# A new written-out order and a three-piece last store in an attention and token/channel-mixer kernel

## The chip, the cores and the metric

The kernel runs on one core of one Trainium2 chip. The metric is the device time of one execution in microseconds; three runs of a version give a median.

## The reference

Blockwise causal attention over 8 batches, 8 heads, 576 positions and 64 channels, followed by a mixer: a token part that multiplies along the positions, and a channel part that multiplies along the 512 channels, each with a residual.

```python
scores = scale * np.matmul(q, k.transpose(0, 1, 3, 2))       # masked by blocks of 64
attn = np.exp(scores - max); attn = attn / (sum + 1e-09)
x = np.matmul(attn, v)                                       # heads side by side: (8, 576, 512)
h = np.maximum(x.transpose(0, 2, 1) @ w_tok1, 0.0) @ w_tok2
u = x + h.transpose(0, 2, 1)
out = u + np.maximum(u @ w_ch1, 0.0) @ w_ch2
```

## The kernel before

The kernel is built in two steps. First the Python code adds about 1,500 numbered operations to a plan; an operation is a bundle of instructions on one engine with its dependencies and, for matmuls, the PSUM banks that it takes. Then the string `ORDER` is walked word by word, and each word emits one operation. A word is a number, an engine letter (T is TensorE, A ScalarE, D VectorE, P GpSimd, S SyncE) and the letters of the banks taken: `41Ta` is operation 41 on TensorE in bank a. Each engine works through its own words in the order written and stops at the first whose inputs or bank are not there. So `ORDER` is the whole schedule. An operation that may run on one of two engines (an evacuation of PSUM on ScalarE or VectorE, a clearing on VectorE or GpSimd) gets its engine from the word too.

What the operations do, by number, so far as they are spoken of below:

- 0A loads the exponential's table. 1D to 6D fill parts of the value tiles, 8D and 9D parts of the token weights, 7D fills `zeros` (part of the tile that the profile calls `wd_sb`), all at L339.
- 41T is eleven matmuls on `zeros`, 512 columns each (L364), which need 7D. 42T to 78T are single matmuls on `zeros` (L372) whose results nobody reads; 42, 46, 50 and so on to 78 have 256 columns, the others 512. Only those that `ORDER` names are emitted. They need 7D and a free bank.
- 11S and 14S load the two halves of the first keys by SyncE's queue, 12A and 15A cast them, 13D and 16D transpose them. 18D, 20D and 22D transpose the three parts of the first queries.
- Batch 0 has its own form of attention: the score sets 98T, 105T, 122T, 102T, 158T, 142T, 125T, 162T, 138T, 145T, 165T (L562) write pairs of banks called s and t (98T two single banks more), and one exponential on 1024 columns (L580) empties a pair: 99A, 106A, 123A, 103A, 159A, 143A, 126A, 163A, 139A, 146A, 166A. 118A and 119A (L736) empty the two single banks of 98T. When 166A has run, the pairs' space turns into four single banks e to h.
- The heads' products with the values are L616 (107T to 175T for batch 0) and L669 (the last 64 positions, 155T for instance); VectorE divides them by the sums (L642, L697).
- Batch 1 begins with the score sets 202T, 208T and 241T in single banks, each emptied by four exponentials of 512 columns (L777). 202T takes banks b, e, f, g.
- Later batches' queries, keys and values come by GpSimd's queue (L417, L469) and are transposed on VectorE (L440). 355P is a load of values, 519P and 522P load four heads' keys and queries of batch 3, 520D and 521D transpose the first. 201 and 240 clear parts of an exponential's result (L599), 240 after the exponentials 236 to 239. 258T is a product with its division 259D and 260D; 426T is the token product of that batch.
- The channel part runs in `channel_up_half`, `channel_up_fast` and `channel_down_fast` with seven products in place of eight (L1114, L1238, L1372); VectorE adds what the banks hold to `o_sb` (L1396), and stores follow at L1438 by SyncE's queue, or ScalarE's for the last batch.

In `channel_down_fast` a batch is worked in one go (`joint`), but the last in two halves of its token chunks, `c0 == 0` and `c0 == 1`. `row` is one of the two rows of `o_sb`, and `h0:h1` says which of the two column halves a store takes. The last operation of `ORDER` before is 1503S, a store of both column halves of one row for `c0 == 0`; the product 1500T and the addition 1501D stand right ahead of it.

Of the kernel before, what the change touches and what calls it, by code (L numbers as in the profile page):

```python
# [27 lines left out]
class Plan:  # L28
# [78 lines left out]
    272D 285Tg 280A 276D 195Tedcf 198A 197A 4D 282D 5D 286D 283Th 284D 310Ta 319Tg 287Th 288A 316Td 295Tc 317T 318D  # L107
    320T 196A 243A 322Th 323T 321A 199A 228Tdbeg 324A 200D 289Tf 207D 290T 232A 230A 261D 296T 297A 6D 345D 311T
    312D 231A 191P 229A 192P 301Tb 193P 262D 346P 302T 235Tcghe 239A 291A 236A 292Td 293T 233D 190P 194P 201P 344D
    304Te 294D 305T 348D 234D 298Tc 299T 347D 352P 216Td 219Tf 220D 237A 303A 217D 218D 213Tb 222Tg 306A 214D 223D  # L110
    300A 238A 215D 240D 225Tc 226D 224D 367Tdhea 370A 227D 221D 313Tb 314T 369A 255Tc 315D 373Tfgeh 246Tb 368A 247D
    376A 307Td 308T 354D 377A 256D 248D 257D 375A 91P 249Te 250D 251D 334Th 371A 360Tcbag 364A 309D 263D 374A 92P
    372D 338Te 339T 335T 349P 362A 353D 252Tb 350D 361A 351D 363A 258Ta 393Tcfgd 397A 395A 396A 93P 336T 355P 264D
    253D 259D 260D 254D 394A 426Tb 427A 406Tagfd 337D 519P 522P 409A 521D 428Tc 340T 410A 407A 520D 400Tadfb 429A
    430Tc 408A 523D 356P 325Tg 94D 341D 358P 359P 402A 524D 431D 365P 366P 404A 357P 384Tb 385D 387Tc 95D 440Td 441A
    381Te 403A 525P 386D 326T 401A 388D 534P 528P 378Tb 389D 379D 390Td 536Tcafh 540A 537A 382D 383D 391D 380D 392D
    434Te 405P 435D 529D 539A 327T 432Td 549Tbfec 433D 685P 552A 398P 399P 553A 328D 438Th 551A 423Td 424D 425D 538A
    436Tg 437D 442Tc 526D 688P 533P 329Td 443A 446Tg 444Tc 417Ta 96D 418D 531P 411Tf 330T 412D 550A 413D 530D 445A
# [60 lines left out]
def kernel(  # L179
# [1148 lines left out]
    def channel_down_fast(b, g_done, wc2_ready, u_done, prio):  # L1328
        gt, ut = g_of(b), u_of(b)
        joint = b != B - 1  # L1330
# [12 lines left out]
        for ts in ((0, 1),) if joint else ((0,), (1,)):  # L1343
            c0, nt = ts[0], len(ts)
# [90 lines left out]
            pieces = [(0, 0, 2), (1, 0, 2)] if c0 == 0 else [(0, 0, 2), (1, 1, 2), (1, 0, 1)]  # L1435
# [151 lines left out]
```

## Time and profile before

| | |
|---|---|
| median of three runs | 285.12 us |
| lowest, highest | 284.26 us, 285.19 us |
| the profiled execution, its own time | 285.85 us |
| its span in the profile | 284.1 us |
| TensorE busy, share of the span | 277.7 us, 98% |
| VectorE busy | 242.4 us, 85% |
| ScalarE busy | 176.0 us, 62% |

The profile's span goes from the first to the last instruction of the program; the profiled execution's own time has 1.75 us more around it. In a timeline row the first number is the start in microseconds, the second the length, then engine, line, operation, what is written and read, and how many such instructions stand together; brackets tell the idle time ahead of it and what ended that. Several matmuls in one row overlap, so the row's length is the spacing of all but the last plus the whole latency of the last. PEld is the loading of weights for a matmul, and an engine's name with a q is its queue of instructions.

### The profile page before, as it was taken

Reading aid. Unit: us, or ns where it says so; the run is one execution under the profiler, and the core shown is the slowest. Engines: PE = TensorE matmul, PEld = TensorE weight load, DVE = VectorE, ACT = ScalarE, POOL = GpSimd, SP = SyncE. Lnnn points to the kernel's source line nnn. Section 1 sums busy time; section 2 is a strip of 40 time slices with the busy share of each in tenths; the row PEclk is TensorE's granted clock in tenths of the full one; section 3 lists DMA queues with packets and bytes.
Section 4 is the critical chain, followed back from the end, with each engine's and each line's share of the span. In section 5 each row is a group of like instructions: output and inputs, shape, how many; then the busy total and the mean of one; then the engine's idle time right before and its main releaser. Section 6 shows DMA issues by size and latency. Waiting matters only on the chain.

```text
span 284.1 us, 8556 instructions
## 1 busy us (share of the span) xinstructions
PE 277.7 (98%) x3586; PEld 194.4 (68%) x3586; DVE 242.4 (85%) x527; ACT 176.0 (62%) x320; POOL 80.2 (28%) x133
## 2 busy tenths in 40 slices
PE   7999999999999999999999999999999999999994
PEld 2457665567767876887777649744488755788883
DVE  4579598889999999989988999879996979889884
ACT  3697896768798666798979891244545774530000
POOL 8876563633742313092552320000000000000000
PEclk9999999999999999999999999999999999999999
DMA  8999999969959578499999827020123600012264
GB/s 158 164 166 196 189 202 206 167 88 111 147 71 166 115 134 105 76 116 87 161 98 253 71 41 96 29 66 18 37 39 71 227 0 1 2 74 95 103 152 171
DMA packets 64773, 31.74 MB, mean 112 GB/s; under 512 B 53088, under 2 KB 55904, under 8 KB 64736
## 3 DMA queue, kind: packets, MB, share of 16 engines
q0 software_dynamic: 45040, 17.64, 53.7%
q1 hardware_dynamic: 19408, 13.05, 17.7%
q8 instruction: 28, 0.46, 0.6%
q10 hardware_dynamic: 288, 0.52, 0.5%
q14 instruction: 9, 0.07, 0.1%
HBM read 35.85 MB, written 9.44 MB: 159 GB/s over the span
## 4 chain that ended last, share of the span: by engine, by line
PE 89%; DMA 6%; POOL 1%; DVE 1%; issue 1%; ACT 1%; POOLq 0%
PE mm L1372 17%; PE late L1372 9%; PE mm L1238 7%; PE late L1114 7%; PE mm L1114 7%; PE late L1238 6%; PE mm L562 5%; PE late L616 4%; PE late L562 3%; PE mm L814 3%; PE mm L616 3%; PE late L1463 3%; PE mm L1041 3%; DMA gT<-in_k_dram 2%; PE mm L913 2%; PE late L814 2%
## 5 line engine op out<-in xcount | busy, mean ns | idle before, releaser
L777 ACT ACTIVATE e_sb<-late 128x512 bf16<-128x512 f32 x85 | 48.4, 609 | 11.5 <-PE late L562 7.3
L777 ACT ACTIVATE e_sb<-mm 128x512 bf16<-128x512 f32 x83 | 47.5, 607 | 7.7 <-PE mm L562 3.3
L440 DVE STREAM_TRANSPOSE qk_sb<-qk_sb 128x288 int32<-128x288 int32 (+2 forms) x57 | 37.0, 693 | 4.5 <-ACT qk_sb L393 1.9
L469 POOL DMA_DIRECT2D vals<-in_v_dram x45 | 37.1, 838 | 7.7 <-DMA wc_sb<-in_moe_w_ch_dram 2.5
L1372 PEld LDWEIGHTS <-gT 128*128 128x128 bf16 x288 | 27.8, 98 | 4.6
L1372 PEld LDWEIGHTS <-sums 128*128 128x128 bf16 x288 | 27.8, 98 | 4.0 <-DVE gT L1354 0.4
L562 PE MATMUL mm<-qk_sb 32*64 32x320 bf16 (+6 forms) x462 | 26.8, 274 | 0.6 <-issue 0.6
L562 PEld LDWEIGHTS <-qk_sb 32*64 32x64 bf16 (+1 forms) x1024 | 16.8, 100 | 15.0 <-issue 9.8
L616 PEld LDWEIGHTS <-e_sb 128*128 128x128 bf16 x640 | 23.5, 97 | 4.4 <-issue 1.1
L562 PE MATMUL late<-qk_sb 32*64 32x320 bf16 (+6 forms) x454 | 25.2, 276 | 0.0
L1114 PEld LDWEIGHTS <-ws_sb 128*128 128x128 bf16 x192 | 18.0, 98 | 3.9 <-issue 0.9
L599 POOL MEMSET e_sb<- 64x512 bf16 (+1 forms) x22 | 11.4, 522 | 29.2 <-ACT e_sb L777 19.0
L1114 PEld LDWEIGHTS <-wc_sb 128*128 128x128 bf16 x144 | 15.5, 114 | 1.5
L1238 PEld LDWEIGHTS <-ws_sb 128*128 128x128 bf16 x96 | 9.4, 98 | 9.7
L1372 PE MATMUL mm<-wd_sb,sums 128*128 128x256 bf16 x126 | 15.6, 273 | 0.0
L616 PE MATMUL late<-vals,e_sb 128*128 128x65 bf16 x330 | 14.4, 193 | 0.0
L642 DVE TENSOR_TENSOR x_sb<-late,rinv 128x256 bf16<-128x256 f32 x33 | 13.6, 419 | 0.7
L580 ACT ACTIVATE e_sb<-sc 128x1024 bf16<-128x1024 f32 x11 | 10.8, 1030 | 5.2 <-PE sc L562 5.0
L616 PE MATMUL mm<-vals,e_sb 128*128 128x65 bf16 x310 | 13.8, 193 | 0.0
L800 ACT ACTIVATE gT<-late 128x512 bf16<-128x512 f32 x18 | 10.6, 606 | 5.0 <-PE late L1114 2.8
L393 ACT COPY late<-mm 128x512 f32<-128x512 f32 x16 | 9.2, 578 | 7.2 <-PE mm L1238 3.7
L642 DVE TENSOR_TENSOR x_sb<-mm,rinv 128x256 bf16<-128x256 f32 x31 | 12.6, 415 | 0.5
(202 smaller groups left out, 645.7 us busy)
## 6 DMA issues: line engine op xcount, KB each, us to landing
out_dram<-o_sb SPq DMA_DIRECT2D x14, 512.0 KB, 3.3
vals<-in_v_dram POOLq DMA_DIRECT2D x28, 128.0 KB, 5.3
qk_sb<-in_k_dram POOLq DMA_DIRECT2D x12, 288.0 KB, 4.9
qk_sb<-in_q_dram POOLq DMA_DIRECT2D x12, 288.0 KB, 5.1
wc_sb<-in_moe_w_ch_dram POOLq DMA_DIRECT2D x8, 192.0 KB, 7.6
wc_sb<-in_moe_w_ch_dram POOLq DMA_DIRECT2D x3, 512.0 KB, 9.2
out_dram<-o_sb SPq DMA_DIRECT2D x5, 256.0 KB, 2.0
vals<-in_v_dram POOLq DMA_DIRECT2D x15, 64.0 KB, 4.9
```

Source lines behind the costliest of these rows:

```text
L440: nc.vector.transpose(dst[:, 0:S, :] .rearrange("p s e -> p (s e)") .bitcast(I32) .rearrange("p (a k) -> p k a", k=NB)[:, k0:k1], raw2.bit ...
L469: nc.gpsimd.dma_start(out=t[128 - p : 128, J, hs, 0:64], in_=src)
L562: nc.tensor.matmul(out=home(n)[rows, c : c + w], lhsT=kT[i][r, 64 * j : 64 * j + keys, par], rhs=qT[i][r, 64 * q : 64 * q + w, par], start ...
L580: nc.scalar.activation(dst, sc[SC.index(note["pool"])][:, :, 0:n], EXP, scale=scale)
L599: (nc.vector if o.engine == "DVE" else nc.gpsimd).memset(late_keys, 0.0)
L616: nc.tensor.matmul(out=u[:, I, 0:65], lhsT=e[:, h, c : c + 128], rhs=vt[:, J, head, 0:65], start=(J == 0), stop=(J == I),)
L642: nc.vector.tensor_tensor(out=xt[:, 0:4, 64 * head : 64 * head + 64], in0=u[:, :, 0:64], in1=ri[:, 0:4].to_broadcast([128, 4, 64]), op=MULT,)
L777: nc.scalar.activation(dst, bank_of(x), EXP, scale=scale)
L814: nc.tensor.matmul(out=ps, lhsT=w1_sb[:, c, tt : tt + 255 : 2], rhs=xt[:, c, cols], start=(c == 0), stop=False)
L1114: nc.tensor.matmul(out=bank_of(bank)[:, 256 * o_ : 256 * o_ + 256], lhsT=x(o_, m), rhs=y[:, :, m, :], start=opens, stop=m == 1, skip_group ...
L1238: nc.tensor.matmul(out=bank_of(bank), lhsT=x(m), rhs=y[:, :, m, :], start=first and m == 0, stop=m == 1, skip_group_check=not first,)
L1372: nc.tensor.matmul(out=bank_of(bank)[:, 256 * i : 256 * i + 256], lhsT=x[:, kk, 128 * i : 128 * i + 128], rhs=y[:, kk], start=first and i ...
```

## The change

The condition for storing in three pieces now holds for both halves of the last batch, not for its second alone. That adds one operation to the plan (1504), and the numbers behind it move up by one: what was 1504 to 1524 is now 1505 to 1525. The last store is now the new 1504A, one column half (the one that 1501D adds), by ScalarE's queue; the other column half of that row goes earlier as 1503S.

`ORDER` is new from end to end. 7D stands ahead of the other fills. It names 23 of the single matmuls on `zeros`, where it named 31: ten with 256 columns and 13 with 512, against ten and 21. All other TensorE operations are the same ones, in another sequence. The core of the edit is in these lines (the first stretch up to the second score set of batch 1, the stretch with 240P, and the end):

```diff
-    9D 8D 14S 7D 0A 15A 11S 41Ta 19P 69Tb 17P 1D 52Tb 21P 31P 25P 51Tb 65Tb 23P 29P 48Tb 56Tb 12A 27P 3D 2D 16D 20D
-    18D 22D 43Tb 13D 26D 24D 105Ts 106A 98Ttbc 61Td 57Td 49Td 99A 100D 30D 63Td 118A 122Ts 70Td 123A 78Td 62Td 54Td
-    102Tt 103A 45Td 28D 64Td 104D 67Td 35P 34P 50Td 33P 158Ts 159A 142Tt 143A 32P 74Td 181P 178P 101D 55Td 115Td
-    68Tb 125Ts 107Tb 184P 108T 116D 117D 124D 183D 119A 162Tt 182D 160D 47Td 179D 40P 126A 59Td 37P 42Td 109D 111Td
-    112T 120D 121D 163A 66Tc 138Ts 180D 145Tt 110D 39P 113D 144D 38P 36P 139A 135Tc 136D 114D 79P 127Ta 128T 131Tb
-    132T 133D 165Ts 80P 140D 82P 161P 53Td 141D 146A 60Td 147Td 137D 129D 130D 166A 151Tc 152T 148T 134D 46Ta 44Ta
-    202Tabef 206A 204A 205A 164D 185D 175Tg 153D 154D 155Th 149D 176D 177D 156D 58Tc 157D 267Tc 268D 150D 203A 265Tg
-    167Th 208Tcebf 266A 187P 168T 81P 88P 87P 84P 83P 171Tg 89P 210A 269Td 209A 270A 90P 172T 211A 86P 85P 212A 343P
-    188D 273Te 189D 169D 170D 186D 277Th 173D 241Tdbca 245A 174D 271Tg 10P 274D 244A 242A 275Te 281Ta 278D 279Th
...
-    1492Tb 1478T 1514T 1507D 1479D 1483S 1487D 1510T 1489D 1512Tc 1511D 1494T 1482A 1515D 1518T 1495D 1490T 1513D
-    1519D 1523S 1516T 1493D 1517D 1522S 1491D 1496T 1498T 1520T 1497D 1502S 1499D 1521D 1524S 1500T 1501D 1503S
+    11S 7D 14S 0A 15A 41Ta 19P 8D 1D 17P 21P 78Tb 31P 48Tb 49Tb 6D 25P 54Tb 45Tb 23P 29P 2D 3D 9D 16D 56Tb 20D 57Tb
+    44Tb 12A 13D 51Tb 22D 18D 26D 98Tsbc 99A 105Tt 59Td 122Ts 100D 24D 106A 118A 30D 47Td 102Tt 123A 52Td 42Td 101D
+    27P 103A 28D 62Td 35P 34P 43Td 119A 33P 55Td 158Ts 142Tt 32P 104D 115Td 116D 159A 160D 111Tc 181P 53Tb 112T 113D
+    143A 114D 120D 121D 125Ts 126A 107Tb 117D 182D 46Ta 74Ta 162Tt 163A 178P 179D 180D 108T 164D 109D 138Ts 184P
+    183D 110D 50Td 139A 40P 37P 39P 38P 36P 124P 140D 127Td 145Tt 4D 131Ta 128T 165Ts 146A 166A 129D 79P 58Tc 132T
+    80P 141D 130D 135Tc 66Tb 70Tb 144D 155Td 133D 134D 202Tbefg 136D 151Ta 152T 205A 204A 161P 203A 137D 186D 156D
+    157D 175Tc 176D 206A 177D 153D 147Th 148T 149D 82P 208Tdfec 211A 209A 212A 185D 167Tb 154D 187P 150D 168T 265Tg
+    267Th 269Ta 266A 210A 189D 5D 270A 188D 171Tc 172T 169D 173D 241Tgfde 268D 244A 243A 242A 10P 81P 88P 273Ta 170D
...
+    296T 313Ta 92P 236A 349P 93P 201P 297A 213Tc 214D 222Td 223D 219Th 216Te 215D 224D 217D 218D 294A 225Tg 367Tcbfd
+    369A 226D 314T 227D 315D 307Tg 308T 368A 370A 220D 221D 373Tecba 377A 374A 376A 309D 240P 249Tf 250D 246Th 251D
+    355P 338Tg 354D 334Tf 335T 375A 261D 255Tc 262D 247D 353D 371A 248D 252Td 253D 339T 256D 257D 360Thbea 361A 254D
+    362A 351D 350D 519P 325Tc 364A 263D 94D 336T 363A 258Td 393Tabhe 394A 395A 259D 520D 260D 326T 397A 340T 426Td
...
+    1495D 1513Th 1516D 1508D 1519T 1482S 1514D 1493D 1520D 1524A 1511T 1512D 1498T 1499D 1503S 1496T 1497D 1517T
+    1518D 1523S 1490T 1521T 1491D 1502S 1522D 1500T 1525S 1501D 1504A
...
-            pieces = [(0, 0, 2), (1, 0, 2)] if c0 == 0 else [(0, 0, 2), (1, 1, 2), (1, 0, 1)]
+            pieces = [(0, 0, 2), (1, 0, 2)] if joint else [(0, 0, 2), (1, 1, 2), (1, 0, 1)]
```

More of the change, by code (lines that the diff above doesn't have):

```diff
@@ L108 @@
[L108 to L117, printed above, removed]
@@ new lines @@
+    666D 814T 917Tadbc 919A 799T 920A 797T 951P 967P 815D 918A 921A 823Td 817T 818A 820Ta 800D 802T 798D 821A
+    884Tcgbe 888A 803A 886A 887A 824D 829T 827T 885A 816D 828D 669Tea 954P 868P 670A 830D 904Tdgfb 906A 908A 953D
+    892Tc 956D 960P 832T 893D 833A 905A 671T 907A 952D 1051P 894D 911Tchbg 955D 1054P 965P 672D 667D 909P 898Td
+    895Te 896D 897D 899D 900D 914A 889Tf 890D 891D 937Tb 966P 901Te 902D 903D 915A 913A 912A 916D 938A 981Tdchg 984A
+    985A 983A 982A 910P 959D 961D 958D 1057P 673Tf 968Teghb 964P 934Tc 962D 935D 936D 971A 1060P 970A 928Td 929D
@@ new lines @@
+    1126D 1127D 1096D 836D 839A 1092Tg 1093D 1094D 1122Td 1123D 1124D 837D 1097D 844T 845D 1268Th 1269D 840T 841D
+    842Tf 843D 1100D 848T 849D 846T 847D 1134D 1091D 1135D 1213Tea 1216A 1153Thd 1156A 850T 1168Tfb 1169Tg 1171A
+    1159T 851D 1136D 1137D 1160A 1214Tc 1215A 1219T 1174T 1175D 1220D 1172Th 1173A 1284Tc 1285D 1154Tf 1155D 784S
+    1176T 1157Te 1170A 1177D 1276Tc 1277D 1282Tf 1217Tc 1158A 1178T 1179D 1283D 1138Thg 1163T 1164D 1218A 1221T
+    1141A 1144T 1161T 1050S 1162D 1223T 1145A 1222D 1142Th 1181T 1182A 1180A 1166T 1198Tce 1167D 1224D 1286Tb 1287D
@@ new lines @@
+    1139Tf 1294Td 1295D 1298S 1143A 1226T 1227A 1140D 1201A 1199Tb 1200D 1290Td 1291D 1146T 1147D 1183Tfa 1148T
+    1184Tb 1185D 1186A 1189T 1190A 1278Th 1279D 1202Td 1187Tf 1272Tb 1203A 1149D 1208T 1274Th 1209D 1188A 1193T
+    1191T 1413D 1273D 1206T 1151T 1152A 852S 1194D 1275D 1204T 1205A 1196T 1197D 1192D 1211T 1212A 1225A 1288Th
+    1207D 1417Tcg 1418Te 1292Tf 1420A 1289D 1432Tda 1433Tb 1293D 1423T 1228D 1229D 1414D 1230D 1231D 1210D 1232Tfh
+    1419A 1236Te 1434A 1237D 1435A 1281S 1233A 1238T 1421Tb 1239D 1234T 1235D 1242T 1422A 1415D 1416D 1240T 1243D
```

104 lines of the change are left out of this document (48 added, 56 removed).

## The prediction

> **What bounds the kernel now.** I read the page first, then who waited for whom on TensorE, then busy time by stretches, then the chain that ended last.
>
> ```profile
> PE 277.7 (98%) x3586; PEld 194.4 (68%) x3586; DVE 242.4 (85%) x527; ACT 176.0 (62%) x320; POOL 80.2 (28%) x133
> ```
> ```profile
> PE mm L364 <- DVE wd_sb L339: 1.7, 1, 1.7
> PE mm L562 <- issue: 0.6, 1, 0.6
> PE mm L372 <- DVE x_sb L642: 0.2, 1, 0.2
> ```
> ```profile
> 8.38:21.94 13.56, 13.56 (x233) 7.31 (x233) 9.13 (x31) 11.49 (x13) 10.89 (x20) 1.00 1.42 167
> 31.13:280.28 249.15, 248.32 (x3131) 177.44 (x3129) 220.36 (x459) 154.32 (x289) 55.68 (x88) 1.00 0.67 104
> ```
> ```profile
> 263.39 3.93 PE mm L1372 x36
> ```
>
> The stretches give length, then busy time of PE, PEld, DVE, ACT and POOL. From 31.13 us to the last matmul's start at 280.28 TensorE is busy 248.32 of 249.15 us, and the chain's row shows what that is worth: 36 matmuls in 3.93 us, 109 ns each, without a hole. So TensorE's stream is the bound there, and its work is the same in both versions. In the first 22 us it is busy too, but partly with matmuls on zeros. Only the start, the tail, and waits that the new sequence makes or removes can move the time.
>
> **The change part by part.** *The first matmul.*
>
> ```profile
> 0.84 0.17 DVE L339 MEMSET w1o_sb<- 64x128 uint32 x1 [0.84 <-PEq L1571]
> 1.33 0.27 DVE L339 MEMSET wd_sb<- 128x256 uint32 x1
> 1.66 4.88 PE L364 MATMUL mm<-wd_sb 128*128 128x512 bf16 x11 [1.66 <-DVE wd_sb L339]
> 6.08 1.50 DVE L440 STREAM_TRANSPOSE qk_sb<-qk_sb 128x288 int32<-128x288 int32 x3 [0.31 <-DMA qk_sb<-in_q_dram]
> 6.33 2.12 PE L372 MATMUL mm<-wd_sb 128*128 128x512 bf16 x7
> 6.76 0.15 PEld L372 LDWEIGHTS <-wd_sb 128*128 128x128 bf16 x1 [0.28 <-issue]
> 7.18 0.77 PEld L372 LDWEIGHTS <-wd_sb 128*128 128x128 bf16 x4 [0.27 <-issue]
> 8.38 0.88 PE L562 MATMUL sc<-qk_sb 32*128 32x512 bf16 x6
> 9.05 1.94 ACT L580 ACTIVATE e_sb<-sc 128x1024 bf16<-128x1024 f32 x2 [4.12 <-PE sc L562]
> 11.06 0.61 PE L372 MATMUL mm<-wd_sb 128*128 128x256 bf16 x4
> ```
>
> VectorE begins at 0.84; 7D started at 1.33 behind two other fills. First in the new order, it starts 0.49 earlier, and so do the eleven matmuls: 1.17 in place of 1.66. They take 6.33 - 1.66 = 4.67 us, so they end at 5.84.
>
> Before the first score set stood seven wide matmuls on zeros (69, 52, 51, 65, 48, 56, 43), after it is seven wide and two narrow ones (78 and 54). Weight loads stand 0.42 us apart up to 7.18 and about 0.21 from there (four in 0.77, the last one 0.15 long): TensorE ran at half its pace until 7.18. A narrow one takes half of a wide one: four in 0.61 with a latency of 0.27 are 0.11 each. If the pace changes at 7.18 again, the new order has four slow ones (0.21 + 0.42 + 0.42 + 0.21 = 1.26, to 7.10) and five fast wide ones (1.05), and reaches the score set at 8.2 to 8.3. If it changes 0.49 earlier with the first matmul, the second narrow one is fast and it is 8.1. Before it was 8.38. The queries' and keys' transposes were all done at 6.08 + 1.50 = 7.58, so data is not late in either. I take 8.2: **-0.2 us** (bounds -0.8, all data there at 7.58, and 0).
>
> The Trainium skill, page "TensorE: Matmul & The Clock Gate", section "What's actually happening", says that the full clock comes after a busy window of about 3.4 us and that these windows run freely. By that the step need not move with the first matmul, and the score set would come at 8.3 at the latest; the row's 5.5 us of slow spacing from 1.66 to 7.18 lie between one and two such windows.
>
> *Batch 0.* Here ScalarE has the longer work.
>
> ```profile
> L580 ACT ACTIVATE e_sb<-sc 128x1024 bf16<-128x1024 f32 x11 | 10.8, 1030 | 5.2 <-PE sc L562 5.0
> 13.74 1.94 ACT L580 ACTIVATE e_sb<-sc 128x1024 bf16<-128x1024 f32 x2 [0.43 <-PE sc L562]
> 15.57 0.60 ACT L736 ACTIVATE e_sb<-mm 128x512 bf16<-128x512 f32 x1
> 18.50 3.10 ACT L580 ACTIVATE e_sb<-sc 128x1024 bf16<-128x1024 f32 x3 [0.49 <-PE sc L562]
> 20.91 0.77 PE L616 MATMUL mm<-vals,e_sb 128*128 128x65 bf16 x20
> 21.94 0.37 PE L562 MATMUL mm<-qk_sb 32*128 32x448 bf16 x2
> 22.68 0.60 ACT L777 ACTIVATE e_sb<-late 128x512 bf16<-128x512 f32 x1 [1.08 <-PE late L562]
> 22.68 0.29 PE L669 MATMUL late<-vals,e_sb 128*64 128x65 bf16 x8
> 23.23 0.27 PE L372 MATMUL mm<-wd_sb 128*128 128x256 bf16 x1 [0.23 <-DVE x_sb L642]
> ```
>
> Eleven wide exponentials, two of which take 1.94 (so 0.92 from one to the next), and two narrow ones of about 0.5 net are 11 x 0.92 + 2 x 0.5 = 11.1 us. They took from 9.05 to 18.50 + 3.10 = 21.60, 12.55 us; the holes are in brackets (0.43, 0.49), the rest is smaller ones. In the new order 119A, whose bank is full since 98T, comes ahead of 159A, where the first hole was, and 138T follows 108T without the four matmuls on zeros (47, 59, 42, 66) that stood between. After the first score set stand 14 matmuls on zeros (six wide, eight narrow) where there were 24 (14 wide, ten narrow): 6 x 0.21 + 8 x 0.11 = 2.1 us against 14 x 0.21 + 10 x 0.11 = 4.0. So TensorE alone would be ready for 202T 1.9 us sooner and more, but 202T needs the banks that 166A sets free. Its end: first score set at 8.2, its 0.7 to the exponential (9.05 - 8.38; 98T is the longer set, but by under 0.1), 11.1 of exponentials and 0.4 for what is left of the holes give 20.4, and 202T starts at about 20.5 in place of 21.94: **-1.4 us**, of which 0.2 is the term above. Bounds: 20.0 with no hole; 21.7 with all of them.
>
> TensorE owes something at that point: 147, 151, 152 and 148 (the row of 20 matmuls at 20.91, 0.6 net) now come after 202T, 155 (0.2 net, as the row at 22.68) before it, and 58 with its wait (0.11 + 0.23) is gone from behind it. That is 0.6 - 0.2 - 0.34, nothing.
>
> *Batch 1's first sets.* 208T now follows with two token products fewer ahead of it, 241T with two products fewer, and each needs things that come late next: 208T the second exponential of 202T, 241T the transposes 189D and 188D, which stand behind 154D and 150D.
>
> ```profile
> 23.18 0.59 ACT L777 ACTIVATE e_sb<-mm 128x512 bf16<-128x512 f32 x1
> 24.78 1.25 DVE L440 STREAM_TRANSPOSE qk_sb<-gT 128x288 int32<-128x288 int32 x2
> ```
>
> 202T's first exponential came 0.74 after it, the second ended at 23.77, 1.83 after 202T. Between the starts of 202T and 208T TensorE has 202T itself (0.6 of those 0.74) and 151, 152, 175, 147 and 148 (0.6 for the 20 matmuls, 0.3 for 175): 0.3 us of waiting. Two transposes take 1.25; of them I reckon 0.2 uncovered at 241T. **+0.5 us** together; bounds 0 and 1.2, in which case all of the lead is given back.
>
> *The stretch behind.* 3131 matmuls in both. TensorE lacks 0.83 us there (249.15 - 248.32); a new sequence can win that or lose as much again. I take 0, bounds -0.8 and +0.8.
>
> *The tail.*
>
> ```profile
> 280.47 0.42 DVE L1396 TENSOR_TENSOR o_sb<-mm,e_sb 128x256 f32<-128x256 f32 x1 [0.25 <-PE mm L1372]
> 280.93 0.33 SPq L1438 DMA_DIRECT2D out_dram<-o_sb  x1
> out_dram<-o_sb SPq DMA_DIRECT2D x1, 256.0 KB, 2.0
> out_dram<-o_sb SPq DMA_DIRECT2D x1, 128.0 KB, 1.7
> out_dram<-o_sb SPq DMA_DIRECT2D x2, 512.0 KB, 2.8
> out_dram<-o_sb ACTq DMA_DIRECT2D x2, 256.0 KB, 4.4
> ```
>
> The last store waits for 1501D in both; it is now 128 KB in place of 256: 1.7 us to landing against 2.0. It goes by ScalarE's queue, which is empty then. The only rows of both queues are pairs sent together, 2.8 and 4.4 us with unlike sizes; if that were the queue's own price the tail would be up to 1.3 longer. The pairs shared the engines and the last store is alone, so I am nearer to the SyncE row: **-0.1 us** (bounds -0.3 and +1.3). The added store is covered: 1503S no longer waits for 1501D, and 1500T's six matmuls run beside it.
>
> Sum: -1.4 + 0.5 + 0 - 0.1 = **-1.0 us**, so a span of 283.1 and an own time of 285.85 - 1.0 = 284.85 for an execution like the profiled one. That one was 0.73 above the median of 285.12; off the median the same sum gives **284.1 us**.
>
> **The rivals.** *The holes come back.* A score set waits for its pair of banks, set free by the exponential two before, and the exponential waits for the set. If TensorE stands in a product of heads at that moment (the 0.77 row), ScalarE waits. Then ScalarE's end stays near 21.4, and the removed matmuls turn into idle time of TensorE: start -0.2, tail -0.1, **284.8 us**. For it: the holes of before were all of that kind. Against it: 119A's new place, and fewer matmuls on zeros to stand in.
>
> *TensorE is not the bound at all.* If its 98% hid slack, evacuations would set the end, dropping matmuls on zeros would give nothing, and the time would be **285.1 us**. The row of 36 in 3.93 speaks against it. The Trainium skill, page "Perfetto Trace Analysis", section "Identifying the Most-Contended Engine", says just that matmul busy time misleads and that weight loads' busy share should be used; here that would be 68% and not 98%.
>
> *A load behind a clearing holds VectorE (slower).*
>
> ```profile
> qk_sb<-in_k_dram POOLq DMA_DIRECT2D x1, 288.0 KB, 11.6
> 40.43 0.56 POOL L417 DMA_DIRECT2D qk_sb<-in_k_dram  x1
> 52.25 0.29 DVE L697 TENSOR_TENSOR x_sb<-mm,rinv 128x128 bf16<-128x128 f32 x1
> 53.95 1.78 DVE L440 STREAM_TRANSPOSE qk_sb<-qk_sb 128x288 int32<-128x288 int32 x3
> ```
>
> On GpSimd 240P is new ahead of 355P, 519P and 522P; it waits for four exponentials of batch 1, so that 519P goes out some 3 us after the 40.43 of before. It landed 11.6 us after its issue, at 52.0, behind other loads. On VectorE 520D now stands between 259D and 260D (260D was the row at 52.25, and the transposes began at 53.95, behind it). If 519 lands late, 520D holds 260D and all evacuations behind it, and 426T, with 393T, 326T and 340T as cover (a set of 0.6 and eight wide matmuls of 0.21, 2.3 us), runs dry. It decides from a landing later than about 54. If all 3 us come through (55.0), that costs 1 us for 519 and as much again for 522, whose transpose follows: -1.0 + 2.1, **286.2 us**. Against it: the loads ahead kept the queue full, so a later issue should wait less and land at the same time.
>
> That the edit does less than it says I leave out: `joint` is false for the last batch alone, so the pieces change there only.
>
> **How the numbers follow.** Less than 0.3% (0.86 us) is about what a measurement of this kernel can tell from no change. Chances: forecast 0.48 (own range 283.2 to 284.25), the holes 0.28, no bound 0.10, the held VectorE and other new waits of its size 0.14. So faster 0.48, same 0.38, slower 0.14. The low end is the forecast with the bounds of the second hole-free chain (-0.4) and the stretch behind (-0.8): 282.9. The high end takes in both middle cases and the held VectorE at half its price, 285.7; its full price is left out.
>
> **What would show it.** In the profile after: the first matmul at 1.17 and the first score set at 8.1 to 8.3; the last wide exponential ending at about 20.4, with TensorE waiting for ScalarE ahead of 202T; 202T near 20.5; 260D not waiting for a landing; from the last addition to the end of the span 0.1 to 0.3 us less. The prediction is wrong if the exponentials still end after 21, if the first score set is not before 8.38, or if TensorE's idle time behind 31 us grows by more than 0.8 us.

## The result, and the profile after

The change made the kernel slower: 285.58 us (284.99 to 286.52, 20 runs) against 284.59 us (283.94 to 285.19, 20 runs) of the kernel before beside it. The ratio is 1.0036 with a 95% interval of 1.0026 to 1.0046, so about 1.0 us was lost where 1.0 us of gain was forecast. A second time it was 285.85 against 284.46 us, ratio 1.0045 (1.0027 to 1.0064). Of the loss 0.25 us stands outside the profile's span: there it is 2.0 us by the medians after and 1.8 before.

The profiled execution of after took 285.61 us, with a span of 283.6. That of before, shown ahead of the prediction, turned out long (285.85, span 284.1): repeated, the same kernel had a profiled 284.77 with a span of 283.0. Where two traces are compared below, the second one of before is used.

The page of after, its list of what TensorE waited for, and its busy time by stretches (length, then busy time of PE, PEld, DVE, ACT and POOL, the granted clock, the share of the DMA engines and GB/s):

```profile
PE 276.1 (97%) x3558; PEld 194.1 (68%) x3578; DVE 242.4 (85%) x526; ACT 175.9 (62%) x322; POOL 79.4 (28%) x132
```
```profile
PE mm L364 <- DVE wd_sb L339: 1.2, 1, 1.2
PE sc L562 <- ACT e_sb L580: 0.6, 1, 0.6
PE late L1041 <- DMA wc_sb<-in_moe_w_ch_dram: 0.3, 1, 0.3
PE mm L669 <- DVE x_sb L642: 0.2, 1, 0.2
```
```profile
8.10:20.45 12.35, 11.38 (x212) 6.81 (x215) 8.70 (x28) 11.19 (x13) 9.99 (x19) 1.00 1.48 169
20.45:30.12 9.67, 9.35 (x215) 7.50 (x212) 7.60 (x26) 8.16 (x18) 6.18 (x11) 1.00 1.03 169
30.12:279.90 249.78, 248.33 (x3121) 177.18 (x3136) 222.26 (x461) 153.83 (x288) 56.20 (x89) 1.00 0.70 105
```

This profile lacks the records of 20 matmuls (3558, against 3578 weight loads), and each missing one looks like idle time, two of them in the first stretch and 18 behind 30 us. So TensorE's 97%, and idle times taken from these rows, can't be compared with before. Three profiles of this order, up to one move, further down have every record (the first ones with two pieces, with the loads ahead of the identity, and with all stores by SyncE). TensorE is busy for 98% there, as before.

Two things are new. In the first stretch TensorE stands idle for about 1 us here (12.35 - 11.38), and for 0.7 to 0.9 us in those three, where before the matmuls on zeros kept it busy all of the time. And a wait has appeared that no list of before had: TensorE for a channel weight (`wc_sb`), a DMA.

The timeline of the head of after, as the prediction had asked for it:

```profile
0.87 0.27 DVE L339 MEMSET wd_sb<- 128x256 uint32 x1 [0.87 <-PEq L1571]
1.20 4.88 PE L364 MATMUL mm<-wd_sb 128*128 128x512 bf16 x11 [1.20 <-DVE wd_sb L339]
5.87 2.30 PE L372 MATMUL mm<-wd_sb 128*128 128x256 bf16 x9
8.10 0.33 PE L562 MATMUL sc<-qk_sb 32*64 32x320 bf16 x2
17.20 2.85 ACT L580 ACTIVATE e_sb<-sc 128x1024 bf16<-128x1024 f32 x3
20.16 0.32 PE L669 MATMUL mm<-vals,e_sb 128*64 128x65 bf16 x8 [0.17 <-DVE x_sb L642]
20.45 0.37 PE L562 MATMUL mm<-qk_sb 32*128 32x448 bf16 x1
```

The first matmul is at 1.20 (forecast 1.17), the first score set at 8.10 (8.1 to 8.3), the wide exponentials end at 20.05 (20.4), and 202T starts at 20.45 (20.5; in before 21.94 in the first profile, 21.48 in the second). So the forecast times of the head were right, and the kernel is slower all the same. That is what the experiments were for.

### The profile page after: what moved, and what is told of

Same layout as the page of the kernel before. It is cut to its first block, busy times and chain, and to the rows that moved or that the text cites. A ratio compares the mean times of both kernels' runs of the same rounds, so it can differ in the third digit from the quotient of the medians.

```text
span 283.6 us, 8524 instructions
## 1 busy us (share of the span) xinstructions
PE 276.1 (97%) x3558; PEld 194.1 (68%) x3578; DVE 242.4 (85%) x526; ACT 175.9 (62%) x322; POOL 79.4 (28%) x132
## 4 chain that ended last, share of the span: by engine, by line
PE 85%; DMA 9%; POOL 2%; issue 1%; DVE 1%; POOLq 0%
PE late L1372 17%; PE mm L1372 9%; PE late L1114 7%; PE mm L1114 7%; PE late L1238 6%; PE mm L1238 6%; PE mm L562 4%; PE late L562 4%; PE late L616 3%; PE mm L616 3%; DMA wc_sb<-in_moe_w_ch_dram 3%; PE late L1463 3%; PE late L814 2%; DMA vals<-in_v_dram 2%; DMA w_sb<-in_moe_w_tok_dram 2%; PE late L913 2%
## 5 line engine op out<-in xcount | busy, mean ns | idle before, releaser
L777 ACT ACTIVATE e_sb<-mm 128x512 bf16<-128x512 f32 x87 | 49.2, 612 | 8.4 <-PE late L562 3.4
L777 ACT ACTIVATE e_sb<-late 128x512 bf16<-128x512 f32 x81 | 46.8, 615 | 12.1 <-PE late L562 7.1
L562 PE MATMUL mm<-qk_sb 32*64 32x320 bf16 (+6 forms) x476 | 28.8, 275 | 0.1
L562 PEld LDWEIGHTS <-qk_sb 32*64 32x64 bf16 (+1 forms) x1024 | 17.4, 99 | 14.8 <-issue 9.4
L562 PE MATMUL late<-qk_sb 32*64 32x320 bf16 (+6 forms) x440 | 26.8, 274 | 0.0
L393 ACT COPY late<-mm 128x512 f32<-128x512 f32 x14 | 8.2, 592 | 13.9 <-PE mm L1238 12.2
L616 PE MATMUL mm<-vals,e_sb 128*128 128x65 bf16 x340 | 15.9, 193 | 0.1
L1372 PE MATMUL late<-wd_sb,sums 128*128 128x256 bf16 x126 | 15.4, 273 | 0.0
L800 ACT ACTIVATE gT<-mm 128x512 bf16<-128x512 f32 x18 | 10.9, 613 | 5.9 <-PE mm L1238 2.2
L642 DVE TENSOR_TENSOR x_sb<-mm,rinv 128x256 bf16<-128x256 f32 x34 | 13.9, 419 | 0.7
L393 ACT COPY mm<-late 128x512 f32<-128x512 f32 x13 | 7.5, 580 | 10.6 <-DVE gT L1153 4.5
L393 ACT COPY mm<-mm 128x512 f32<-128x512 f32 (+1 forms) x7 | 4.0, 568 | 15.8 <-PE mm L1372 14.4
L616 PE MATMUL late<-vals,e_sb 128*128 128x65 bf16 x300 | 13.0, 193 | 0.1
```

What stands on the lines that cost most here:

```text
L393: nc.scalar.copy(dst, src)
L562: nc.tensor.matmul(out=home(n)[rows, c : c + w], lhsT=kT[i][r, 64 * j : 64 * j + keys, par], rhs=qT[i][r, 64 * q : 64 * q + w, par], start ...
L616: nc.tensor.matmul(out=u[:, I, 0:65], lhsT=e[:, h, c : c + 128], rhs=vt[:, J, head, 0:65], start=(J == 0), stop=(J == I),)
L642: nc.vector.tensor_tensor(out=xt[:, 0:4, 64 * head : 64 * head + 64], in0=u[:, :, 0:64], in1=ri[:, 0:4].to_broadcast([128, 4, 64]), op=MULT,)
L777: nc.scalar.activation(dst, bank_of(x), EXP, scale=scale)
L800: nc.scalar.activation(dst, src, RELU)
```

## The experiments

In the diffs, words of `ORDER` that only changed place are shown where they now stand. Theory at the start: the lead of the head is real and something behind it eats it. Rival: the head gains nothing, whatever its clock times say.

**The kernel before, again.** No edit.

> The kernel before, unchanged, for a second profile. The profiled execution of before took 285.85 us, 1.26 above the median of its 20 timed runs (284.59). If that execution was an odd one, this profile has a span near 282.8 and shows where the odd one was longer; if a profile always costs that much, the span is near 284 again. The ratio is 1 within 0.1% in both.

284.56 us, ratio 0.9997 (0.9984 to 1.0011), span 283.0 in its profile. Against the first profile the first score set stands at 7.91 in place of 8.38, and by 1114T it is 1.06 us ahead (166.85 against 167.91). An execution of this kernel differs from the next by up to 1 us at such points.

**The three-piece store alone, on the old order; and the new order with two pieces.**

Each edit also sets the condition of `pieces` as the other version has it, and with it the numbers behind 1503; the diffs show the end of `ORDER` alone.

```diff
-    1502S 1499D 1521D 1524S 1500T 1501D 1503S
+    1502S 1499D 1503S 1522D 1525S 1500T 1501D 1504A
```
```diff
-    1500T 1525S 1501D 1504A
+    1500T 1524S 1501D 1503S
```

> The order of before with the three-piece store alone: the last store is split into 1503S after 1499D and 1504A, by ScalarE's queue, after 1501D. My term of the tail: 0.1 us faster. Rival (the last store on another queue costs outside the span, as the 2.0 us around after's span against 1.75 around before's suggest): 0.2 to 0.4 us slower with the span unchanged. If the whole loss came from here: 1.0 us slower.

> The order of after with the last row stored whole by SyncE (1503S last, two pieces), the rest as in after. If the new sequence has the loss: still 0.7 to 1.0 us slower than before. If the three pieces have it: within 0.3 us of before or faster.

The store alone: 284.95 us, ratio 1.0010 (0.9998 to 1.0023). The new order with two pieces: 285.28 us, ratio 1.0029 (1.0017 to 1.0041), and a second time, beside after on the same chip, 285.77 against its 285.85 (ratios 1.0036, 1.0021 to 1.0052, and 1.0045). So most of the loss is the order. The store is small, and the tails of the traces show its sign. The additions and the store at the end of the second profile of before (span 283.0; two stores stand in its row, the last is issued at its end) and of after (span 283.6), with the sizes and times to landing:

```profile
279.19 1.01 SPq L1438 DMA_DIRECT2D out_dram<-o_sb  x2
279.41 0.42 DVE L1396 TENSOR_TENSOR o_sb<-mm,e_sb 128x256 f32<-128x256 f32 x1 [0.25 <-PE mm L1372]
out_dram<-o_sb SPq DMA_DIRECT2D x1, 256.0 KB, 2.0
```
```profile
280.10 0.42 DVE L1396 TENSOR_TENSOR o_sb<-late,e_sb 128x256 f32<-128x256 f32 x1 [0.23 <-PE late L1372]
280.55 0.34 ACTq L1438 DMA_DIRECT2D out_dram<-o_sb  x1
out_dram<-o_sb ACTq DMA_DIRECT2D x1, 128.0 KB, 1.7
```

The store of 128 KB lands 0.3 us sooner after its issue, as forecast. But from the last addition's start to the end of the execution (283.0 - 279.41 and 283.6 - 280.10 in the span, and what lies around it, 1.8 us in before and 2.0 in after by the medians) it is 3.6 + 1.8 = 5.4 us before and 3.5 + 2.0 = 5.5 after; the store alone on the old order gives 3.8 + 1.9 = 5.7. The 2.0 is not the store's, since the new order with two pieces has it as well; that order takes 3.4 us from the addition to the end of the span in four profiles with two pieces, and 3.5 in five with three. Like with like, nothing of the 0.3 comes through, and 0.1 to 0.3 us is lost. The Trainium skill, page "SBUF — State Buffer", section 'The DMA setup-cost knee (why "@ 1 MiB" ≠ asymptote)', says that every transfer pays about 2 us that do not depend on its bytes, mostly the wait for its completion. The landings of 1.7 and 2.0 us for 128 and 256 KB are near that, and by it a smaller last store could not bring much.

> The kernel after, with the last of the three stores issued by SyncE (1504S) and not by ScalarE. If ScalarE's queue costs the 0.3 us, the stretch from the last landing to the end of the span falls from 1.35 to about 0.95 and the median to 285.3. If it is the number of stores, or the landing of 128 KB, the end stays 4.3 to 4.4 us behind the start of 1500T and the median within 0.15 of 285.58.

```diff
-    1500T 1525S 1501D 1504A
+    1500T 1525S 1501D 1504S
```

285.71 us, ratio 1.0039 (1.0019 to 1.0058), 3.5 us from the last addition to the end of the span as in after. From the landing to the end of the span it is 1.36 us here and 1.35 in after, and 0.9 in the same order with two pieces. So ScalarE's queue is not the cause; the third piece is, though why the end of the program follows it later no run here shows.

**Fewer matmuls on zeros; the fill first.**

```diff
-    60Td 61Td 63Td 64Td 65Tb 67Td 68Tb 69Tb
```
```diff
-    9D 8D 14S 7D 0A
+    7D 9D 8D 14S 0A
```

> The order of before without the eight matmuls on zeros 60, 61, 63, 64, 65, 67, 68, 69 that after leaves out. My theory: TensorE is ahead sooner, but ScalarE's exponentials set 202T, so 0.2 to 0.8 us faster. Rival: the holes in ScalarE's row stay and nothing is won, ratio 1 within 0.1%.

> The kernel before, with one move on VectorE: fill 7D ahead of 9D and 8D, so that the first matmuls on zeros wait for one fill. The first matmul comes at 1.20 in place of 1.66. If the step to the faster pace follows the first matmul, the first score set comes 0.3 to 0.5 us sooner than its 7.91 (limited by the transposes, which are done at about 7.6); if it runs by a clock of its own, within 0.1 us of 7.91 to 8.4. Batch 0 is bound by ScalarE, so 202T moves with the first score set by 0 to 0.3 us, and the median is 284.3 to 284.6. If the order of the fills makes the 0.25 us outside the span, own time less span is 2.03; if not, 1.78.

Without those eight: 284.47 us, ratio 0.9992 (0.9978 to 1.0007). With the fill first: 284.37 us, ratio 0.9994 (0.9979 to 1.0010), and a second time 284.72, ratio 0.9998 (0.9984 to 1.0012). Neither is a gain that can be told from none. In the two profiles of the kernel with the fill first, the same program, the first score set stands at 7.63 and at 8.10. The rows of weight loads show from when they stand 0.2 us apart, and no longer 0.43:

```profile
5.75 1.18 PEld L372 LDWEIGHTS <-wd_sb 128*128 128x128 bf16 x6 [0.16 <-issue]
7.63 0.88 PE L562 MATMUL sc<-qk_sb 32*128 32x512 bf16 x6 [0.20 <-DVE qk_sb L440]
```
```profile
7.14 0.53 PEld L372 LDWEIGHTS <-wd_sb 128*128 128x128 bf16 x3 [0.26 <-issue]
8.10 0.88 PE L562 MATMUL sc<-qk_sb 32*128 32x512 bf16 x6
```

So the step to the faster pace does not follow the first matmul: it comes at about 5.7 and at 7.1 us with the same first matmul at 1.20. The score set moves less than the step, because in the first profile it waits for the transposes. The Trainium skill, page "TensorE: Matmul & The Clock Gate", section "What's actually happening", says that the windows of the clock gate run freely and that the step therefore varies by half a microsecond either way. That it varies these traces show too, but by more: 1.4 us between these two.

**The loads ahead of the identity.** In the new order GpSimd builds the identity (10P) ahead of 81P, a load of token weights, and the loads of channel weights behind it; before, 10P stood behind all of them.

```diff
-    243A 242A 10P 81P 88P 273Ta
+    243A 242A 81P 88P 87P 84P 83P 89P 90P 86P 10P 273Ta
```

> The kernel after, with one move on GpSimd: the eight loads 81P, 88P, 87P, 84P, 83P, 89P, 90P and 86P go out ahead of the identity (10P) and not behind it; every other engine has the same instructions in the same order. Theory W (the weight loads of batch 0 land too late for the earlier products): 81P is issued at about 19.2 in place of 19.7 us and lands at 25.0 to 25.5 in place of 26.27, 85P at 33.0 to 33.5 in place of 34.45; TensorE's waits at 273T (0.41), 277T (0.30) and 299T (0.48) shrink to under 0.15 each, 228T starts at 34.5 to 34.8 in place of 35.48, and the median falls by 0.7 to 1.0 us, from 285.58 to 284.6 to 284.9. Theory O (the loss is the sequence itself, which has other work late there, and the landings only happen to come then): the landings move, 273T or 299T then wait for VectorE or ScalarE instead, and the median stays within 0.3 us of 285.58.

285.28 us, ratio 1.0012 (0.9994 to 1.0030). That is 0.3 us under after by the medians, which were not taken beside each other, and 0.7 by the ratios. Repeated beside after on the same chip:

> The kernel after, once more, beside the next two on the same chip: ratio 1.003 to 1.0045, median 285.4 to 285.8. Its first profile had 0.48 us of waiting at 299T for a channel weight that landed at 34.45 us; in two other profiles of this order the load landed at 34.08 and 32.53 and nothing waited there. If the wait is the rule, this profile shows it again.

> The eight loads ahead of the identity, a second time. If the order of the loads is worth 0.3 to 0.7 us, the median lies that much under the kernel after beside it, 284.9 to 285.3. If the first result (1.0012 against 1.0036) was chance, it lies within 0.15 us of it.

> The kernel after with two pieces, a second time. By the tails of the traces the third piece costs 0.1 to 0.3 us, so the median lies 0.1 to 0.3 us under the kernel after beside it. If the forecast of a gain of 0.1 us from the third piece was right, it lies 0.1 us above.

After: 285.85 us. With the loads ahead: 284.97 us, ratio 1.0015 (1.0005 to 1.0025). That is 0.9 us for one move on GpSimd, every other engine's instructions being the same in the same order. The same move with two pieces, in the next experiment, goes from ratios of 1.0029 and 1.0036 to 1.0014. GpSimd's and TensorE's rows of the second profile of after, then of the kernel with the loads ahead:

```profile
19.62 0.21 POOL masks.py:197 MEMSET ident<- 128x128 bf16 x1
19.90 0.29 POOL masks.py:199 TENSOR_SCALAR_AFFINE_SELECT ident<-ident 128x128 bf16<-128x128 bf16 x1
20.14 0.55 POOL L480 DMA_DIRECT2D w_sb<-in_moe_w_tok_dram  x1
20.69 3.71 POOL L503 DMA_DIRECT2D wc_sb<-in_moe_w_ch_dram  x7
27.02 1.07 PE L849 MATMUL mm<-aT,w_sb 128*128 128x128 bf16 x16 [0.95 <-DMA w_sb<-in_moe_w_tok_dram]
35.21 0.62 PE L1041 MATMUL late<-uT,wc_sb 128*128 128x512 bf16 x2 [0.61 <-DMA wc_sb<-in_moe_w_ch_dram]
```
```profile
19.29 0.54 POOL L480 DMA_DIRECT2D w_sb<-in_moe_w_tok_dram  x1
19.82 3.19 POOL L503 DMA_DIRECT2D wc_sb<-in_moe_w_ch_dram  x6
26.13 0.62 PE L849 MATMUL mm<-aT,w_sb 128*128 128x128 bf16 x8
27.04 0.61 PE L849 MATMUL mm<-aT,w_sb 128*128 128x128 bf16 x8 [0.28 <-DVE x_sb L642]
33.56 1.03 PE L1041 MATMUL late<-uT,wc_sb 128*128 128x512 bf16 x4
```

273T (the L849 row) waits 0.95 us for 81P, and 299T (the L1041 row) 0.61 us for 85P; with the loads ahead both waits are gone. 81P is issued at 20.14 against 19.29 and lands at 26.98 against 25.76; 85P lands at 35.16 against 32.87. It is not so in every execution. In five profiles with the identity ahead, 81P lands at 24.85 to 26.98, and in four of them 273T starts within 0.05 us of that landing; in the same four 299T starts within 0.06 us of the landing of 85P. In six profiles with the loads ahead (two of them of kernels that have another order further back), that is so at 273T twice (26.43 and 26.51, landings 26.39 and 26.46) and at 299T once. So the wait comes and goes from one execution to the next, and with the identity ahead it comes more often. The issue of 81P wanders too, between 19.0 and 20.2 us with the identity ahead and 18.5 and 20.1 without; what else moves it, no run here shows. A start at the landing need not cost much (with two pieces, first profile, TensorE is idle for only 0.07 us in all from 30.12 to 277 us). And the identity's place is not the whole of it: before, 299T stood at 39.8 to 40.5 us, and the new order has it at 34 to 35, so the same load has 6 us less. The expected 0.7 to 1.0 us was right in the second pair of runs and, by the medians, high in the first.

**On top of it, two pieces; then VectorE's order.** In the kernel with the loads ahead, 277T still waits 0.3 us for a bank that 170D empties, and 170D stands behind 173D, at which VectorE stands idle (first profile):

```profile
26.25 0.18 DVE L636 RECIPROCAL rinv<-mm 128x4 f32<-128x4 f32 x1 [0.93 <-ACT aT L800]
26.35 0.39 DVE L802 TENSOR_SCALAR aT<-late 128x256 bf16<-128x256 f32 x1
26.66 0.74 DVE L642 TENSOR_TENSOR x_sb<-mm,rinv 128x256 bf16<-128x256 f32 x2
```

> The same move on GpSimd, and the last batch's rows stored in two pieces, as before the change. Theory W together with the price of 0.3 us for the third piece: 0.3 us under the kernel with the move alone, 284.3 to 284.6, level with the kernel before or up to 0.3 us under it, because the time outside the span stays 0.25 us longer. Theory O: 285.0 to 285.3.

```diff
-    169D 173D 241Tgfde 268D
+    169D 170D 268D 173D 241Tgfde
```

> The kernel with the loads ahead of the identity and two pieces, with one more move, on VectorE alone: 170D and 268D, which are ready, stand ahead of 173D and not behind it. There VectorE stands idle for 0.93 us until 26.25 with 173D at its head, and 277T waits for the bank that 170D empties. Theory V (this queue order is what eats the lead of the head at 26 to 28 us): 277T's wait of 0.29 to 0.44 goes to under 0.1, the first products after it start 0.3 us sooner, and the median falls by 0.2 to 0.4 us, from 284.98 to 284.6 to 284.8. Theory L (what is late at 277T is the work itself: 273T, 271T and batch 1's exponentials come next): the wait moves to the next product, and the median stays within 0.15 of 284.98.

Two pieces: 284.98 us, ratio 1.0014 (0.9998 to 1.0030). That is the expected 0.3 us under the move alone by the medians, but not by the ratios, and it misses the expected 284.3 to 284.6. With 170D and 268D ahead as well: 284.60 us, ratio 1.0005 (0.9994 to 1.0016), level with before. VectorE now has its work ahead of the idle time:

```profile
25.29 0.42 DVE L642 TENSOR_TENSOR x_sb<-mm,rinv 128x256 bf16<-128x256 f32 x1
25.63 0.41 DVE L802 TENSOR_SCALAR aT<-late 128x256 bf16<-128x256 f32 x1
25.96 0.17 DVE L636 RECIPROCAL rinv<-mm 128x4 f32<-128x4 f32 x1
27.32 1.29 DVE L862 TENSOR_TENSOR u_sb<-mm,x_sb 128x512 bf16<-128x512 f32 x2 [0.73 <-PE mm L849]
```

277T's wait is gone, as Theory V says. The addition behind it still starts at 27.32, as in the first profile of the kernel with the loads ahead, because in this execution 273T started at 26.51 with the landing of 81P. The medians have Theory V's size, but with these intervals a step of 0.4 us is not settled. Three mends later the new order is level. The forecast gain is still missing.

**The head alone.** The new head up to 241T (with the two mends), and from there the old order.

```diff
     86P 85P 343P
-    188D 273Te 189D 169D 170D 186D 277Th 173D 241Tdbca 245A
+    273Te 277Th 241Tdbga 245A
```

> The order of the kernel with 170D moved up to 241T (25.7 us), and from there the whole order of the kernel before, with two pieces: the head of the change alone. Theory H (202T comes 0.7 to 1.0 us sooner, but TensorE has done the same needed work at 20 us in both orders and then waits 1.4 us between 20 and 28 us, against 1.0 to 1.4 in the order of before, so the earlier head is worth nothing behind it): the start of 228T is within 0.3 us of its 33.74 to 33.96 of before, and the median is 284.3 to 284.7. Theory G (the lead of the head is real and is lost only by what the new order does later): 228T starts at 32.8 to 33.2 and the median is 283.5 to 283.9. In both, new waits at the seam near 26 us would be seen in the trace.

> The head up to 241T before the old order, a second time, beside the kernel with the fill first. Theory G' (the head alone is worth about half of what was forecast, 0.4 to 0.8 us): the ratio is 0.997 to 0.9985 again, the median 0.2 to 0.5 us under the kernel with the fill first. If the first result was chance: within 0.15 us of the kernel with the fill first, ratio 0.999 to 1. Its profile of the first time had a hole of 0.5 us inside 277T (at 26.4 us) that no engine explains; without it 228T starts at 33.8 and the last product at 277.7.

> The kernel before with fill 7D first, a second time: ratio 0.999 to 1.000, the median 0 to 0.3 us under the kernel before, because batch 0 is bound by the score sets and the exponentials and not by the first matmul.

284.07 us, ratio 0.9979 (0.9965 to 0.9993), and the second time 284.35, ratio 0.9995 (0.9983 to 1.0007), beside 284.72 of the kernel with the fill first. The first median lies between the two theories, the second in the range of Theory H; against the kernel with the fill first the second is 0.4 us faster, as Theory G' has it, while its ratio is the one that was named for chance. The mean of the two is 0.13% or 0.4 us, and the second alone is not a gain that can be told from none. This is the fastest order here, but it is not shown to beat before.

The traces say more than the medians, since from 241T on the two orders are the same and 228T stands behind the same needed products. 202T and 228T of the head alone (second profile), then of the kernel with the fill first (second profile):

```profile
20.25 0.37 PE L562 MATMUL mm<-qk_sb 32*128 32x448 bf16 x1
33.80 0.33 PE L562 MATMUL mm<-qk_sb 32*64 32x320 bf16 x2
```
```profile
21.66 0.37 PE L562 MATMUL mm<-qk_sb 32*128 32x448 bf16 x2
34.24 0.33 PE L562 MATMUL mm<-qk_sb 32*64 32x320 bf16 x2
```

| start, us | 202T | 241T | 228T |
|---|---|---|---|
| old head (as before, with three pieces, with the fill first, with fewer zeros), six profiles | 21.19 to 21.97 | 26.56 to 27.31 | 33.74 to 34.48 |
| new head, two profiles | 20.25, 20.75 | 26.62, 27.17 | 33.80, 34.35 |

At 202T the new head leads by 0.4 to 1.7 us; at 241T and 228T it stands inside the old head's range. The 32.8 to 33.2 of Theory G is reached by neither: the forecast lead is gone 6 us later, with nothing of the new order behind it. Two profiles in a range of 0.7 us do not exclude a few tenths.

The same can be counted with more profiles. Give each product the shortest time to the next product's start that it took in any trace here; what a stretch has over the sum of these is time that its products did not need. Up to 228T that is 13.2 to 14.0 us in seven profiles of the old head, 13.3 and 13.9 in the two here, 13.4 to 13.7 in five of the new order with the loads ahead, and 13.8 to 14.8 in five with the identity ahead. From the first score set to 202T the new head saves 0.3 to 0.9 us of it. Between 202T and 228T it spends as much: 1.5 to 1.6 us here, 1.3 to 1.6 in the order with the loads ahead, against 0.8 to 0.9 behind the old head.

**The other seams.** The new order up to 228T (35 us) and up to 400T (53 us), then the old one.

```diff
     199A 200D 312A
-    228Thfda 192P 289Te
+    295Tc 228Tdbeg 289Tf
```
```diff
     356P 264D 407A
-    400Tgdcf 401A 402A
+    400Tadfb 430Tc 402A
```

> The same head with the new order kept up to 228T (35 us), and from there the order of before. The stretch from 26 to 35 us is then the new one with its two mends, and what comes behind is that of before. Theory S (the new order's later part has about 0.5 us more of short waits behind 60 us): 0.3 to 0.5 us under the 284.60 of the kernel with 170D moved, so 284.1 to 284.3. The rival (equal but for chance): 284.5 to 284.7. The traces are to show the waits between 60 and 140 us at 2.5 us and not at 3.1.

> The order of that last kernel up to 400T (about 53 us), and from there the order of the kernel before, with two pieces. Theory S (the new sequence behind 60 us has more short waits at the switches between kinds of product: 4.3 us that the products do not need, against 3.8 in the order of before, by the spacing of the products in the traces): the median falls by 0.4 to 0.6 us more, to 284.0 to 284.4, level with or a little under the kernel before. Rival: those waits are equal in both but for chance, and the median stays within 0.2 of the kernel with 170D moved. The time outside the span is 1.78 if the later part of the order makes it, and 2.03 if the first 53 us do.

285.97 us, ratio 1.0038 (1.0021 to 1.0055), and 287.32 us, ratio 1.0094 (1.0078 to 1.0110). The mirror image, the kernel with the fill first up to its 400T and the new order from there, with two pieces, took 286.11 us, ratio 1.0062 (1.0048 to 1.0076), where 284.8 to 285.0 was expected if the later part of the new order has more waits, and 284.2 to 284.5 if not. All three miss their expectation, because the seam itself stalls. TensorE's longest wait behind the seam in each of the three, in that order:

```profile
35.53 0.59 PE L1041 MATMUL mm<-uT,wc_sb 128*128 128x512 bf16 x2 [0.69 <-ACT gT L800]
```
```profile
61.71 0.76 PE L616 MATMUL mm<-vals,e_sb 128*128 128x65 bf16 x20 [0.81 <-ACT e_sb L777]
```
```profile
62.78 0.59 PE L913 MATMUL mm<-aT,w_sb 128*128 128x512 bf16 x2 [1.16 <-DVE x_sb L642]
```

So what the new order's later part costs is not measured. The spacing of the products gives a hint, by the count that was used for the head. From 60 to 140 us the time that the products did not need is 2.1 to 2.5 us wherever that part has the old order, behind the first of these seams too, and 2.8 in all nine profiles that have the new one throughout. That this is what the medians lose is argued, not shown.

## Why the prediction was wrong

The clock times of the head came out, and none of their worth. What failed is the step from a sooner start to time won: two products that were put off behind 241T were not counted, and a train of loads that goes out later was not seen. Point by point:

- **The first matmul**, -0.2. It came at 1.20 and the score set at 8.10, in the forecast range. But the same program puts that score set at 7.63 or 8.10, so the 0.2 is less than what one execution differs from the next, and the fill moved alone gave ratios of 0.9994 and 0.9998. That 8.10 fell into the range is partly luck: the step to the faster pace wanders by more than the cases lie apart that the prediction worked out.
- **Batch 0**, -1.4. The clock times were right and what they are worth was not. The exponentials end at 20.05 and 202T starts at 20.45, as worked out, but a start that comes sooner was booked as time won. Ahead of 202T the old order had 147, 148, 151 and 152 done. The prediction did count these (0.6 - 0.2 - 0.34, nothing), but it set against them 0.34 us for 58T and its wait, in a place where the new order has waits of its own (0.54 us between 202T and 208T that the products do not need, against 0.43 in the second profile of before). At 20.0 us after and the second profile of before have both started 8.2 us of needed products. Of the matmuls on zeros that the new order leaves out, much stood in time in which TensorE had nothing else to do: 0.7 to 0.9 us came back as idle time.
- **Batch 1's first sets**, +0.5, bounds 0 and 1.2. This is the step that failed. The waits were sized about rightly: between 202T and 241T the time that the products do not need is 0.96 us in after and 0.55 in the second profile of before. But the prediction said that two products fewer stand ahead of 241T, and did not add them again: 273T and 277T are needed work, and a TensorE that reaches 241T without them still owes them behind it. In the second profile of before 241T started 0.99 us after 273T:

```profile
25.80 1.05 PE L849 MATMUL late<-aT,w_sb 128*128 128x128 bf16 x16
26.79 0.41 PE L562 MATMUL mm<-qk_sb 32*128 32x512 bf16 x4
```

241T came 1.2 us sooner than there (25.60 against 26.79); less 0.99 that is 0.2. Against the first profile of before (27.29) it is 0.7, and behind 241T come more waits, even with the loads ahead: up to 228T 0.5 to 0.7 us that the products do not need, against 0.2 in the old order. So the head's -0.9 is about 0. The named upper bound, "all of the lead is given back", came true, but for work that was put off and not for the waits that it was meant for.
- **The stretch behind**, 0. Its bounds of 0.8 were wide enough: in the three profiles that have every record TensorE is idle for 0.07 us between 30.12 and 277 us, against 0.54 in the second profile of before, and the longest wait seen there, in the second profile of after, was the 0.61 at 299T. (The rows of after and of before would give 1.45 against 0.83, but the first counts missing records.) What the sum left out stands ahead of it, between 241T and 31 us: 273T's wait of 0.95. The second step that failed is this omission: the identity, 10P, moved on GpSimd from behind the loads 81P to 85P and 343P to ahead of them, while 299T, which needs 85P, moved 6 us forward. The prediction looked at 240P ahead of 519P on the same queue and not at this move. 0.9 us in the runs beside each other, 0.3 by medians or 0.7 by ratios in the first comparison.
- **The tail**, -0.1. The landing was sized rightly (1.7 us) and the end did not follow it: +0.1 to +0.3, inside the bounds of -0.3 and +1.3, on the other side. The landing was taken for the end of the program, and the stretch from the landing to the end (1.35 us with the third piece, 0.9 with two in the same order) was put at no change.

Together: the head 0 in place of -0.9, the loads +0.3 to +0.9, the third piece +0.1 to +0.3, and about +0.25 outside the span, which comes with the new order whatever its store and which no term of the sum had. That gives +0.65 to +1.45 against a measured +1.0 and, the second time, +1.4. What sets the 0.25, and whether the later part of the order has a share, stays open.

Of the rivals, the holes did not come back (exponentials done at 20.05). The load 519P did not hold VectorE: in the first profile of after it went out 3.1 us later than in the first profile of before (43.49 against 40.43) and landed 1.5 later, at 53.51, ahead of the 54 at which the prediction saw it decide. In after 520D and 260D follow without idle time, each row here starting before the one ahead has ended:

```profile
54.17 0.69 DVE L440 STREAM_TRANSPOSE qk_sb<-qk_sb 128x288 int32<-128x288 int32 x1
54.70 0.28 DVE L697 TENSOR_TENSOR x_sb<-mm,rinv 128x128 bf16<-128x128 f32 x1
```

The mechanism of that rival, a load issued later on GpSimd's queue and a consumer that then waits, is the one that happened, 20 to 27 us sooner and with other loads. "TensorE is not the bound" was half right: not for the whole kernel, where TensorE stays busy for 98%, but in the head, where dropping eight matmuls on zeros gave a ratio of 0.9992 (0.9978 to 1.0007). The rule of the Trainium skill, page "Perfetto Trace Analysis", section "Identifying the Most-Contended Engine", that matmul busy time misleads, had its point there: TensorE was busy for 13.56 of 13.56 us in that stretch of before, and weight loads for 7.31. The page's reason is that matmuls are pipelined; what misled here were matmuls that nobody needs, and the weight loads' share counts those too.

## What to carry to other kernels

Where an engine fills its gaps with work that nobody needs, its busy share says nothing; ask how much needed work is done by a given moment, and book a start that comes sooner only by what has not been put off to behind it. When an order is rewritten, go through every queue, the DMA issuing ones first: half a microsecond of other work ahead of a train of loads went with waits of 0.95 and 0.61 us 7 and 15 us later, where the consumers had moved forward as well. Mending that one place brought back 0.3 us of the 1.0 that was lost the first time, by the medians, and 0.9 of the 1.4 the second time.

## What the runs showed of the hardware

- Issued 0.85 us later, 0.5 of it the identity's, 81P landed 1.2 us later and 85P 2.3 us later (20.14, 26.98 and 35.16 against 19.29, 25.76 and 32.87). 85P, eight loads further back on the queue, goes out 0.28 to 0.29 us after the landing of 81P in all 20 profiles (at 27.26 and 26.04 in these two), so a delay of the first load is passed on.
- The same program, twice, has its step to the faster pace 1.4 us and its first score set 0.47 us apart, and in the first profile of the head alone TensorE had a hole inside 277T that no engine explains:

```profile
26.67 0.56 PE L849 MATMUL late<-aT,w_sb 128*128 128x128 bf16 x7 [0.33 <-issue]
```

- The time around the span is not a constant. By the medians it is 1.8 us with the old order and two pieces, 1.9 with the old order and three pieces, with the new head up to 241T alone and with the new order from 400T on alone, and 2.0 to 2.05 with the new order, whether it goes up to 228T, to 400T or to the end; no run here shows what sets it.
